# Loading the sixth wo column through 40 partitions in two groups of each layer

## The chip, the cores and the metric

The kernel runs on one core of a Trainium2 chip. The metric is the device time of one execution in microseconds (us); of several executions the median is taken. The profile is of one execution.

## What is computed

Two layers, with the same weights and caches in both. Each adds an attention over the last 4096 cached positions (one query, 32 heads of 192) and then a mixer and MLP to a vector of 640 numbers. The part that matters here is the attention and its output projection:

```python
W = min(4096, max(256, Sk // 4))                    # 4096
q = (x @ wq).reshape(B, Sq, Hq, Dh)                 # 1 x 640 @ 640 x 6144
scores = einsum("bhqd,bhkd->bhqk", q, k[-W:]) * Dh ** -0.5
o = einsum("bhqk,bhkd->bhqd", softmax(scores), v[-W:])
return o.reshape(B, Sq, Hq * Dh) @ wo               # 1 x 6144 @ 6144 x 640

x = x + attention(layernorm(x)); x = x + mixer(layernorm(x))   # layer 0
x = x + attention(layernorm(x)); x = x + mixer(layernorm(x))   # layer 1
```

## The kernel before

All data is bf16. The heads are worked off in eight groups of four (layer 0 from the last group to the first, layer 1 from the first to the last). Each head has a K and a V of 1.5 MB, each loaded by one transfer of 128 rows of 12,288 bytes (`load_k`, `load_v`). A group's part of wo is 768 rows of 640 numbers, 960 KB: partition p gets six consecutive rows of wo, 7,680 bytes, and so holds six columns of 640 numbers beside each other (`load_wo`, L161 to L169). All these land in eleven cells of SBUF. In layer 0 seven cells are gradually kept for the transposed K of heads 0 to 6, which layer 1 uses again.

Every load is issued by SP, in one order that is written out beforehand (`layer_stream`, L205 to L244): the K of the next group and the V of this one in turn, after them the group's wo, at the end of a layer w3 and w4 of the mixer. A load waits for its cell to be free and for one of eight DMA semaphores, so that at most eight transfers are in flight.

For a head, VectorE transposes K in quarters (L377), TensorE forms the scores (L453); after a group's four heads comes a softmax over all four (`softmax_steps`, L473 to L540), then TensorE multiplies with V (`pv`, L569), VectorE turns the result (L576), and `o_fold` (L578 to L589) leaves the group's outputs in `oT`, 128 partitions by six columns, which fit the six columns of wo.

The output projection of a group is done one group later, in the middle of the next softmax. In five groups of layer 0 and four of layer 1 it is done by `out_row` (L608 to L627): for each of the six columns two matmuls with one column of oT as weights and half a wo row as moving data, into rows 0 and 32 of a PSUM tile; `add` then adds these to a running sum `acc` in SBUF (L623, L625), and once per layer `turn_row` (L629 to L639) turns that row into a column. The other groups go through `out_proj` (L591).

The steps around it are in this order (`attention`, L766 to L801): T of the next head, `part_max`, T, S, `turn_max`, `full_max`, S, `spread_max`, the query projection of the group after next, `out_row`, `turn_p`, T, the rest of that projection, `add`, `swap` (the transposed probabilities PT, L523). The engines TensorE, VectorE, ScalarE and SP run in exactly this program order. Small PSUM tiles come from a pool of two buffers (`psm`), so a tile waits for the last reader of the tile but one before it.

Ahead of all that, 66 small matmuls (`WARM`, L77 and L310) run on TensorE, and constants are built: `ident`, `ones` (128 x 128, L264), `Lq` and others. The input x is loaded by one transfer of five partitions of 256 bytes (L127).

Of the kernel before, what the change touches and what calls it, by code (L numbers as in the profile page):

```python
# [8 lines left out]
BF16 = mybir.dt.bfloat16  # L9
F32 = mybir.dt.float32  # L10
# [7 lines left out]
P = 128  # L18
# [17 lines left out]
def kernel(  # L36
# [14 lines left out]
    nc = tc.nc  # L51
    _, _, D = A_x.shape
    _, H, Sk, Dh = A_k_cache.shape
# [20 lines left out]
    NA = Dh // 32  # L74
    NKX = 6
    NKEEP, NCELL = 7, 11
    WARM = 66  # L77

# [6 lines left out]
    assert W4C % 2 == 1 and W4C < NF  # L85
    GROUPS = [[list(range(h, h + QH)) for h in range(0, H, QH)] for _ in range(2)]
    GROUPS[0].reverse()

    head = ctx.enter_context(tc.tile_pool(name="head", bufs=1))
    fixed = ctx.enter_context(tc.tile_pool(name="fixed", bufs=1))  # L90
# [66 lines left out]
    def load_wq(layer, kc):  # L157
        nc.sync.dma_start(wq_sb[:, kc, :], A_wq[kc * P:(kc + 1) * P, :])
        return wq_sb

    def load_wo(layer, c):  # L161
        t = take(("wo", layer, c))
        src = A_wo[c * QC:(c + 1) * QC, :].rearrange("(p c) n -> p (c n)", c=NA)
        parts = {NG - 2: (3, 3), NG - 1: (3, 2, 1)}.get(c, (NA,)) if layer == 1 else (NA,)
        i = 0
        for n in parts:
            nc.sync.dma_start(t[:, i * D:(i + n) * D], src[:, i * D:(i + n) * D])
            i += n
        return t  # L169
# [91 lines left out]
        out=ident[:], in_=ident[:], compare_op=ALU.not_equal, fill=1.0,  # L261
        base=0, pattern=[[-1, P]], channel_multiplier=1,
    )
    ones = const.tile([P, P], F32, name="ones")  # L264
    nc.vector.memset(ones[:], 1.0)
    Lf = wx_sb[:, 0:2 * P].bitcast(F32).rearrange("p (j i) -> p j i", j=4)
    nc.gpsimd.memset(Lf, 0.0)
    for base in (0, -1, -64, -65):
# [22 lines left out]

    Lq = const.tile([P, 32], F32, name="Lq")
    nc.vector.reduce_sum(Lq[:], ident[:].rearrange("p (j a) -> p a j", j=4), axis=AX.X)
    eps1 = head.tile([P, 1], F32, name="eps1")
    nc.vector.memset(eps1[:], eps)

# [25 lines left out]
    def ln_center(x, rowsum):  # L322

        mean_ps = psm.tile([P, 1], F32, tag="psm")
        nc.tensor.matmul(mean_ps[:], lhsT=ones[:], rhs=rowsum[:, 0:1], start=True, stop=True)
        xc = big.tile([P, ND], BF16, name="xc")
        nc.vector.scalar_tensor_tensor(out=xc[:], in0=mean_ps[:, 0:1].broadcast_to([P, ND]), scalar=-1.0 / D,
                                       in1=x[:], op0=ALU.mult, op1=ALU.add)
        xcf = big.tile([P, ND], F32, name="xcf")
        nc.vector.scalar_tensor_tensor(out=xcf[:], in0=mean_ps[:, 0:1].broadcast_to([P, ND]), scalar=-1.0 / D,  # L330
                                       in1=x[:], op0=ALU.mult, op1=ALU.add)
        junk = sm.tile([P, ND], F32, tag="ln_junk")
        ssq = sm.tile([P, 1], F32, tag="ln_ssq")
        nc.scalar.activation(junk[:], xcf[:], ACTF.Square, accum_out=ssq[:, 0:1])

        def total():
            var_ps = psm.tile([P, 1], F32, tag="psm")
            nc.tensor.matmul(var_ps[:], lhsT=ones[:], rhs=ssq[:, 0:1], start=True, stop=True)
            return var_ps

        return xc, xcf, total
# [10 lines left out]
    def row_space(layer):  # L352

        t, i = ((wx_sb, 8 * P), (kx, 0))[layer]
        return t[0:33, i:i + D].bitcast(F32), t[0:33, i + D:i + D + QC // 2]

    kept = {}
    area = [None, 0]
# [114 lines left out]
    def softmax_steps(n, ST_ps, sc):  # L473
# [25 lines left out]
        def spread_max():  # L499
            nb_ps = psm.tile([P, 1], F32, tag="psm")  # L500
            nc.tensor.matmul(nb_ps[:], lhsT=held["w"],  # L501
                             rhs=ones[0:1, 0:1], start=True, stop=True)
            nb_sb = big.tile([P, 1], F32, name="nb_sb")
            nc.scalar.copy(nb_sb[:], nb_ps[:])  # L504
            Pr = o_bytes[:, 0:SW]
            lpart = big.tile([P, 1], F32, name="lpart")
            nc.scalar.activation(out=Pr, in_=ST_ps, func=ACTF.Exp,  # L507
                                 bias=nb_sb[:, 0:1], scale=sc[:, 0:1], accum_out=lpart[:, 0:1])
            held["Pr"], held["l"] = Pr, lpart
# [7 lines left out]
        def swap():  # L517
            ng = NGK // NT
            PT_ps = psm.tile([P, n, NJ4, NGK], F32, tag="psm")
            src = held["PrT"].rearrange("p (g j i) -> p i j g", g=ng, j=NJ4)  # L520
            for m in range(NM):
                for q in range(NT):
                    nc.tensor.matmul(PT_ps[32 * m:32 * (m + 1), :, :, ng * q:ng * (q + 1)], lhsT=Eq[:, q, :],  # L523
                                     rhs=src[:, m:QW:NM], start=True, stop=True)
            PT = big.tile([P, n, NJ4 * NGK], BF16, name="PT")
            nc.scalar.copy(PT[:].rearrange("p h c -> p (h c)"), PT_ps[:].rearrange("p h j g -> p (h j g)"))  # L526
            l_ps = psm.tile([P, QH], F32, tag="psm")
            nc.tensor.matmul(l_ps[:], lhsT=ones[:], rhs=held["lh"][:], start=True, stop=True)  # L528
            held["lps"] = l_ps
            return PT  # L530

# [73 lines left out]
                give(("wo", layer, c))  # L605
        return y_ps

    def out_row(layer, c, oT, acc, first):  # L608

        wo_t = need("wo", layer, c)  # L610
        N = D // 2
        yr_ps = psm.tile([33, N], F32, tag="psm")
        for k in range(NA):
            for i in range(2):
                nc.tensor.matmul(yr_ps[32 * i:32 * i + 1, :], lhsT=oT[:, k:k + 1],  # L615
                                 rhs=wo_t[:, k * D + i * N:k * D + (i + 1) * N], start=(k == 0), stop=(k == NA - 1))
        give(("wo", layer, c))

        def add():
            for i in range(2):  # L620
                r = slice(32 * i, 32 * i + 1)
                if first:
                    nc.vector.tensor_copy(acc[r, :], yr_ps[r, :])  # L623
                else:
                    nc.vector.tensor_add(acc[r, :], acc[r, :], yr_ps[r, :])  # L625

        return add  # L627

    def turn_row(acc):  # L629
        y_ps = psm.tile([P, ND], F32, tag="psm")  # L630
        N = D // 2
        for n in range(ND):
            a, b = n * P, (n + 1) * P
            for i in range(2):
                lo_, hi = max(a, i * N), min(b, (i + 1) * N)
                if lo_ < hi:
                    nc.tensor.matmul(y_ps[lo_ - a:hi - a, n:n + 1], lhsT=acc[:, lo_ - i * N:hi - i * N],  # L637
                                     rhs=ident[0:33, 32 * i:32 * i + 1], start=True, stop=True)
        return y_ps  # L639

    def attention(layer, x_cur, rs_cur, x_new, z_new, rs_new, ss_new):
# [29 lines left out]
        def add_y(y_ps, n):  # L671
            y_new = x_new if n == 0 else sm.tile([P, ND], F32, name="y_acc")
            if n == 1:

                rs = big.tile([P, 1], F32, name="rs_y")
                nc.vector.scalar_tensor_tensor(out=y_new[:], in0=y_ps[:], scalar=1.0, in1=y[0][:],
                                               op0=ALU.mult, op1=ALU.add, accum_out=rs[:, 0:1])

                def center():
                    nm_ps = psm.tile([P, 1], F32, tag="psm")  # L680
                    nc.tensor.matmul(nm_ps[:], lhsT=ones[:], rhs=rs[:, 0:1], start=True, stop=True)
# [12 lines left out]
            y[0] = y_new  # L694
# [39 lines left out]
        for gi, cur in enumerate(groups):  # L734
            nxt = list(enumerate(groups[gi + 1])) if gi + 1 < len(groups) else []
            ST_n = None
            if nxt:
# [24 lines left out]
                else:  # L762
# [5 lines left out]
                    part_max()  # L768
                    T(h0, 1)
                    S(h0, 0, ST_n, 0)  # L770
                    turn_max()
                    full_max()
                    S(h0, 1, ST_n, 0)
# [6 lines left out]
                        q[0]()  # L780
                    in_row = gi - 1 in rows
                    if pending is not None:
                        y_ps = out_row(layer, *pending, acc, gi - 1 == rows[0]) if in_row else out_proj(layer, pending)
                    turn_p()
                    T(h1, 0)
                    if q:
# [73 lines left out]
    def mixer(layer, x_cur, z, rs_cur, ss_cur, x_new, rs_new):  # L860
# [2 lines left out]


        s1_ps = psm.tile([P, 1], F32, tag="psm")
        nc.tensor.matmul(s1_ps[:], lhsT=ones[:], rhs=rs_cur[:, 0:1], start=True, stop=True)
        s2_ps = psm.tile([P, 1], F32, tag="psm")
        nc.tensor.matmul(s2_ps[:], lhsT=ones[:], rhs=ss_cur[:, 0:1], start=True, stop=True)
# [119 lines left out]
```

## Time and profile before

| | |
|---|---|
| median of three runs | 520.45 us (519.64 to 520.55) |
| the profiled execution | 519.84 us, its span 518.0 us |
| DMA read from memory | 216.47 MB, 418 GB/s over the span |
| TensorE matmuls, busy | 324.8 us (63%), granted clock 0.70 |
| VectorE, busy | 295.2 us (57%) |
| ScalarE, busy | 49.5 us (10%) |
| wo loads of 960 KB | 13, median 26.5 us from issue to landing |
| wo matmuls in out_row (L615) | 108, in 9 groups of 12 |

The span runs from the first to the last recorded instruction. In the profile PE is TensorE's matmuls, PEld its weight loads, DVE VectorE, ACT ScalarE, POOL GpSimd, SPq the queue of SP, which issues the loads. A line of the chain of waits has start, length and what the time went to; a line of the timeline has start, length, engine, line of the program, operation, what it writes and reads, its shape, how many, and in brackets how long the engine stood idle before it and for whom. A line of the list of waits says who waited for whom: us in total, times, longest. Section 3 of the page lists the DMA queues: q1 carries the data, q8 and q14 instructions.

### The profile page before, as it was taken

How to read it: one execution, taken by the hardware profiler on the slowest of the kernel's cores; microseconds unless marked ns; L12 is line 12 of the kernel's file. 1: busy time of each engine (PE TensorE's matmuls, PEld its weight loads, DVE VectorE, ACT ScalarE, POOL GpSimd, SP SyncE). 2: the span in 40 equal slices, each digit the busy share in tenths (PEclk: the TensorE clock that was granted, in tenths of full speed). 3: DMA queues.
4: the chain of work that ended last, by engine and by line, in shares of the span. 5: the costliest groups of instructions: out<-in, count | busy, mean ns of one | idle time of the engine just before them, and what ended most of it. 6: DMA issues, size and time to landing. Idle time of an engine off the chain costs nothing.

```text
span 518.0 us, 9589 instructions
## 1 busy us (share of the span) xinstructions
PE 324.8 (63%) x4146; PEld 192.6 (37%) x4146; DVE 295.2 (57%) x589; ACT 49.5 (10%) x175; POOL 4.0 (1%) x16
## 2 busy tenths in 40 slices
PE   2057656666664566767755866777566856648665
PEld 2024334333332334434333634434333433425334
DVE  2067667575584655656624356567675765664722
ACT  1000101010010100001011111001010101001011
POOL 2000000000000000000000000000000000000000
PEclk9999878565586755677665778557785676776855
DMA  8999999999999999999999999999999999999995
GB/s 347 433 425 426 433 426 427 432 428 425 433 426 427 431 426 429 428 426 431 424 425 396 385 426 429 428 428 428 429 426 427 432 428 426 426 434 426 427 416 235
DMA packets 23949, 217.08 MB, mean 419 GB/s; under 512 B 2532, under 2 KB 3044, under 8 KB 8420
## 3 DMA queue, kind: packets, MB, share of 16 engines
q1 hardware_dynamic: 23908, 216.48, 99.0%
q8 instruction: 32, 0.52, 0.4%
q14 instruction: 9, 0.07, 0.0%
HBM read 216.47 MB, written 0.00 MB: 418 GB/s over the span
## 4 chain that ended last, share of the span: by engine, by line
DMA 50%; PE 23%; DVE 22%; issue 2%; ACT 1%; SPq 1%; DVEq 0%; ACTq 0%
DMA cell<-in_A_k_cache_dram 39%; DVE cell L377 16%; DMA cell<-in_A_v_cache_dram 9%; PE ST_ps L453 9%; PE O_ps L569 7%; DVE o_sb L576 2%; DMA cell<-in_B_w_dram 2%; DVE pm L478 1%; PE nb_ps L501 1%; DVE o_sb L512 1%; ACT o_sb L507 1%; PE y_ps L637 1%; PE l_ps L528 1%; PE PT_ps L523 1%; PE qT_ps L407 1%
## 5 line engine op out<-in xcount | busy, mean ns | idle before, releaser
L453 PE MATMUL ST_ps<-cell,Qblk 128*16 128x256 bf16 x1536 | 163.7, 380 | 106.9 <-DVE cell L377 69.4
L377 DVE STREAM_TRANSPOSE cell<-cell 128x768 uint32<-128x768 uint32 x228 | 204.1, 945 | 15.2 <-DMA cell<-in_A_k_cache_dram 14.9
L453 PEld LDWEIGHTS <-Qblk 128*16 128x16 bf16 x1536 | 86.1, 111 | 176.5 <-issue 150.3
L569 PE MATMUL O_ps<-cell,PT 128*2 128x384 bf16 x1018 | 99.9, 461 | 8.2 <-DMA cell<-in_A_v_cache_dram 7.4
L576 DVE STREAM_TRANSPOSE o_sb<-O_ps 128x384 f32<-128x384 f32 x64 | 37.2, 581 | 111.8 <-PE O_ps L569 111.6
L569 PEld LDWEIGHTS <-PT 128*2 128x2 bf16 x1024 | 46.0, 100 | 22.1 <-issue 10.1
L512 DVE STREAM_TRANSPOSE o_sb<-o_sb 128x256 bf16<-128x256 bf16 x16 | 7.1, 446 | 33.2 <-ACT o_sb L507 24.2
L584 ACT ACTIVATE oT<-oT_ps,rl 32x6 bf16<-32x6 f32 x40 | 10.3, 258 | 164.0 <-PE oT_ps L583 157.8
L583 PEld LDWEIGHTS oT_ps<-o_sb,Lq 128*32 128x32 f32 x160 | 13.3, 145 | 19.3 <-issue 15.8
L583 PE MATMUL oT_ps<-o_sb,Lq 128*32 128x6 f32 x160 | 13.9, 195 | 10.4 <-DVE o_sb L576 9.9
L589 ACT ACTIVATE oT<-oT_ps,rl 32x6 bf16<-32x6 f32 x24 | 6.2, 258 | 107.6 <-PE ST_ps L453 87.1
L407 PE MATMUL qT_ps<-xc,wq_sb 128*128 128x1 bf16 x210 | 7.1, 165 | 12.8 <-DMA wq_sb<-in_A_wq_dram 12.0
L523 PE MATMUL PT_ps<-o_sb,Eq 128*32 128x32 bf16 x256 | 7.3, 237 | 9.3 <-DVE o_sb L512 4.1
L523 PEld LDWEIGHTS <-Eq 128*32 128x32 bf16 x256 | 5.4, 108 | 19.8 <-issue 19.7
L421 DVE TENSOR_TENSOR Xq<-qT_ps,maskq 128x24 bf16<-128x24 f32 (+1 forms) x18 | 2.8, 158 | 17.1 <-PE qT_ps L407 17.1
L396 PE MATMUL qr_ps<-wq_sb,xc 128*1 128x384 bf16 x90 | 12.1, 415 | 0.0
L407 PEld LDWEIGHTS <-wq_sb 128*128 128x128 bf16 x210 | 6.7, 102 | 14.0 <-DMA wq_sb<-in_A_wq_dram 13.0
L504 ACT COPY nb_sb<-nb_ps 128x1 f32<-128x1 f32 x16 | 2.5, 159 | 94.6 <-PE nb_ps L501 94.6
L615 PE MATMUL yr_ps<-cell,oT 128*1 128x320 bf16 x108 | 11.2, 355 | 0.0
L528 PE MATMUL l_ps<-lh,ones 128*128 128x4 f32 x32 | 7.7, 310 | 4.9 <-ACT PT L526 4.9
L428 PE MATMUL Qrep_ps<-Xq,Lb 128*128 128x24 bf16 (+1 forms) x18 | 3.2, 178 | 11.1 <-DVE Xq L421 10.8
L588 PE MATMUL oT_ps<-o,Lq 128*32 128x6 f32 x48 | 6.1, 199 | 6.5 <-DVE o L587 6.5
(143 smaller groups left out, 200.9 us busy)
## 6 DMA issues: line engine op xcount, KB each, us to landing
cell<-in_A_k_cache_dram SPq DMA_DIRECT2D x57, 1536.0 KB, 26.3
cell<-in_A_v_cache_dram SPq DMA_DIRECT2D x57, 1536.0 KB, 25.8
cell<-in_A_wo_dram SPq DMA_DIRECT2D x13, 960.0 KB, 26.5
wq_sb<-in_A_wq_dram SPq DMA_DIRECT2D x5, 1536.0 KB, 12.2
cell<-in_A_v_cache_dram SPq DMA_DIRECT2D x4, 768.0 KB, 23.8
cell<-in_A_v_cache_dram SPq DMA_DIRECT2D x2, 1248.0 KB, 11.5
cell<-in_B_w_dram SPq DMA_DIRECT2D x1, 1536.0 KB, 11.9
cell<-in_B_w_dram SPq DMA_DIRECT2D x2, 768.0 KB, 10.3
```

What stands on the lines that cost most here:

```text
L377: nc.vector.transpose(Tu, Ku[:, :, q * NY:(q + 1) * NY])
L396: nc.tensor.matmul(qr_ps[32 * i:32 * i + 1, :], lhsT=xc[:, kc:kc + 1], rhs=wq_sb[:, kc, t0 * P + i * N:t0 * P + (i + 1) * N], start=(kc == ...
L407: nc.tensor.matmul(qT_ps[:, tl:tl + 1], lhsT=wq_sb[:, kc, t * P:(t + 1) * P], rhs=xc[:, kc:kc + 1], start=(kc == 0), stop=(kc == ND - 1))
L453: nc.tensor.matmul(ST_ps[r:r + QW, :].rearrange("p (g i) -> p g i", g=ng), lhsT=Q[:, n, :], rhs=T4[:, :, f, :, t], start=(hq == 0 and n == ...
L512: nc.vector.transpose(held["PrT"], held["Pr"])
L523: nc.tensor.matmul(PT_ps[32 * m:32 * (m + 1), :, :, ng * q:ng * (q + 1)], lhsT=Eq[:, q, :], rhs=src[:, m:QW:NM], start=True, stop=True)
L528: nc.tensor.matmul(l_ps[:], lhsT=ones[:], rhs=held["lh"][:], start=True, stop=True)
L569: nc.tensor.matmul(O_ps[r:r + 2, :], lhsT=PT[:, hq, 2 * i:2 * i + 2], rhs=v_pair(V, h, 2 * i * Dh, 2 * Dh), start=(i < 4), stop=(i >= NB - 4))
L576: nc.vector.transpose(o_sb[:], O_ps.rearrange("p (e a c) -> p e c a", e=2, c=NA))
L583: nc.tensor.matmul(oT_ps[r, :], lhsT=Lq[:], rhs=o_sb[:, e, :, e], start=(e == 0), stop=(e == 1))
L584: nc.scalar.activation(oT[r, :], oT_ps[r, :], ACTF.Copy, scale=rl[r, 0:1])
L615: nc.tensor.matmul(yr_ps[32 * i:32 * i + 1, :], lhsT=oT[:, k:k + 1], rhs=wo_t[:, k * D + i * N:k * D + (i + 1) * N], start=(k == 0), stop= ...
```

## The change

Two groups of each layer (the third and fourth in order) get a wo whose sixth column is stored in another way. The first five columns go to all 128 partitions in one transfer as before, now with rows of 6,400 bytes. The sixth column, 128 pieces of 1,280 bytes, goes by two small transfers: 96 pieces to partitions 0 to 23, four beside each other, and 32 pieces to partitions 32 to 47, two beside each other. The sources of these are written with an outer dimension of 6 and of 4.

So that the outputs fit, `spread_low` takes the sixth column of oT through four selection matmuls into a tile of 48 partitions by four columns, and `out_row` then runs five column steps as before, four steps over partitions 0 to 23 and two over 32 to 47, the latter into PSUM rows 64 and 96. `add` has four rows to add, `acc` 97 partitions, and `turn_row` sums the two pairs of rows through `E2`. `ones` becomes one column that is read as a broadcast, and WARM goes from 66 to 14.

```diff
-    WARM = 66
+    WARM = 14
...
+    SPLIT = [{GROUPS[layer][g][0] // QH for g in gs} for layer, gs in enumerate(((2, 3), (2, 3)))]
+    NU = NA - 1
+    LOW = (0, 0, 6, 4), (3 * P // 4, 32, 4, 2)
...
+    def load_wo_split(t, src):
+        nc.sync.dma_start(t[:, 0:NU * D], src[:, 0:NU * D])
+        for row, at, ne, cols in LOW:
+            nc.sync.dma_start(t[at:at + 4 * ne, NU * D:(NU + cols) * D],
+                              src[row:row + 4 * ne * cols, NU * D:].rearrange("(j a) n -> a j n", a=ne))
...
+        if c in SPLIT[layer]:
+            load_wo_split(t, src)
+            return t
...
-    ones = const.tile([P, P], F32, name="ones")
-    nc.vector.memset(ones[:], 1.0)
+    one = const.tile([P, 1], F32, name="one")
+    nc.vector.memset(one[:], 1.0)
+    ones = one[:, 0:1].broadcast_to([P, P])
...
+    Sel = const.tile([P, 4, 48], BF16, name="Sel")
+    nc.gpsimd.memset(Sel[:], 0.0)
+    for row, at, ne, cols in LOW:
+        n = 4 * ne
+        nc.vector.tensor_copy(Sel[:, 0:cols, at:at + n].rearrange("p c (a b) -> p c a b", a=ne),
+                              ident[:, row:row + n * cols].rearrange("p (b c a) -> p c a b", b=4, c=cols))
+    E2 = const.tile([P, 2], F32, name="E2")
+    e4 = ident[:].rearrange("p (s i r) -> p s i r", s=2, i=2)
+    nc.vector.tensor_add(E2[:], e4[:, 0, :, 0], e4[:, 1, :, 0])
...
-        return t[0:33, i:i + D].bitcast(F32), t[0:33, i + D:i + D + QC // 2]
+        return t[0:97, i:i + D].bitcast(F32), t[0:33, i + D:i + D + QC // 2]
...
+    def spread_low(oT):
+        oX_ps = psm.tile([48, 4], F32, tag="psm")
+        for j in range(4):
+            nc.tensor.matmul(oX_ps[:, j:j + 1], lhsT=Sel[:, j], rhs=oT[:, NU:NA], start=True, stop=True)
+        oX = big.tile([48, 4], BF16, name="oX")
+        nc.scalar.copy(oX[:], oX_ps[:])
+        return oX
...
-        yr_ps = psm.tile([33, N], F32, tag="psm")
-        for k in range(NA):
+        yr_ps = psm.tile([33 if oX is None else 97, N], F32, tag="psm")
+        steps = [(0, oT[:, k:k + 1], wo_t[:, k * D:(k + 1) * D]) for k in range(NA if oX is None else NU)]
+        if oX is not None:
+            for _, at, ne, cols in LOW:
+                r = slice(at, at + 4 * ne)
+                steps += [(2 * at, oX[r, j:j + 1], wo_t[r, (NU + j) * D:(NU + j + 1) * D]) for j in range(cols)]
+        at = [r for r, _, _ in steps]
+        for k, (r, o, w) in enumerate(steps):
             for i in range(2):
-                nc.tensor.matmul(yr_ps[32 * i:32 * i + 1, :], lhsT=oT[:, k:k + 1],
-                                 rhs=wo_t[:, k * D + i * N:k * D + (i + 1) * N], start=(k == 0), stop=(k == NA - 1))
+                nc.tensor.matmul(yr_ps[r + 32 * i:r + 32 * i + 1, :], lhsT=o, rhs=w[:, i * N:(i + 1) * N],
+                                 start=r not in at[:k], stop=r not in at[k + 1:])
...
-            for i in range(2):
+            for i in range(2 if oX is None else 4):
...
-                                     rhs=ident[0:33, 32 * i:32 * i + 1], start=True, stop=True)
+                                     rhs=E2[0:97, i:i + 1], start=True, stop=True)
...
                     S(h0, 0, ST_n, 0)
+                    oX = None
+                    if pending is not None and pending[0] in SPLIT[layer]:
+                        oX = spread_low(pending[1])
                     turn_max()
```

More of the change, by code (lines that the diff above doesn't have):

```diff
@@ L324, in ln_center @@
         mean_ps = psm.tile([P, 1], F32, tag="psm")
-        nc.tensor.matmul(mean_ps[:], lhsT=ones[:], rhs=rowsum[:, 0:1], start=True, stop=True)
+        nc.tensor.matmul(mean_ps[:], lhsT=ones, rhs=rowsum[:, 0:1], start=True, stop=True)
         xc = big.tile([P, ND], BF16, name="xc")
@@ L337, in total @@
             var_ps = psm.tile([P, 1], F32, tag="psm")
-            nc.tensor.matmul(var_ps[:], lhsT=ones[:], rhs=ssq[:, 0:1], start=True, stop=True)
+            nc.tensor.matmul(var_ps[:], lhsT=ones, rhs=ssq[:, 0:1], start=True, stop=True)
             return var_ps
@@ L501, in spread_max @@
             nc.tensor.matmul(nb_ps[:], lhsT=held["w"],
-                             rhs=ones[0:1, 0:1], start=True, stop=True)
+                             rhs=one[0:1, 0:1], start=True, stop=True)
             nb_sb = big.tile([P, 1], F32, name="nb_sb")
@@ L527, in swap @@
             l_ps = psm.tile([P, QH], F32, tag="psm")
-            nc.tensor.matmul(l_ps[:], lhsT=ones[:], rhs=held["lh"][:], start=True, stop=True)
+            nc.tensor.matmul(l_ps[:], lhsT=ones, rhs=held["lh"][:], start=True, stop=True)
             held["lps"] = l_ps
@@ L606, in out_proj, with out_row @@
         return y_ps
-    def out_row(layer, c, oT, acc, first):
+    def spread_low(oT):
[5 more added lines that the diff above has]
+        return oX
+    def out_row(layer, c, oT, acc, first, oX=None):
         wo_t = need("wo", layer, c)
         N = D // 2
-        yr_ps = psm.tile([33, N], F32, tag="psm")
-        for k in range(NA):
+        yr_ps = psm.tile([33 if oX is None else 97, N], F32, tag="psm")
[6 more added lines that the diff above has]
+        for k, (r, o, w) in enumerate(steps):
             for i in range(2):
-                nc.tensor.matmul(yr_ps[32 * i:32 * i + 1, :], lhsT=oT[:, k:k + 1],
-                                 rhs=wo_t[:, k * D + i * N:k * D + (i + 1) * N], start=(k == 0), stop=(k == NA - 1))
+                nc.tensor.matmul(yr_ps[r + 32 * i:r + 32 * i + 1, :], lhsT=o, rhs=w[:, i * N:(i + 1) * N],
+                                 start=r not in at[:k], stop=r not in at[k + 1:])
         give(("wo", layer, c))
         def add():
-            for i in range(2):
+            for i in range(2 if oX is None else 4):
                 r = slice(32 * i, 32 * i + 1)
-                if first:
+                if first and i < 2:
                     nc.vector.tensor_copy(acc[r, :], yr_ps[r, :])
@@ L680, in center @@
                     nm_ps = psm.tile([P, 1], F32, tag="psm")
-                    nc.tensor.matmul(nm_ps[:], lhsT=ones[:], rhs=rs[:, 0:1], start=True, stop=True)
+                    nc.tensor.matmul(nm_ps[:], lhsT=ones, rhs=rs[:, 0:1], start=True, stop=True)
                     ym = big.tile([P, ND], F32, name="y_m")
@@ L782, in attention @@
                     if pending is not None:
-                        y_ps = out_row(layer, *pending, acc, gi - 1 == rows[0]) if in_row else out_proj(layer, pending)
+                        y_ps = out_row(layer, *pending, acc, gi - 1 == rows[0], oX) if in_row else out_proj(layer, pending)
                     turn_p()
@@ L865, in mixer @@
         s1_ps = psm.tile([P, 1], F32, tag="psm")
-        nc.tensor.matmul(s1_ps[:], lhsT=ones[:], rhs=rs_cur[:, 0:1], start=True, stop=True)
+        nc.tensor.matmul(s1_ps[:], lhsT=ones, rhs=rs_cur[:, 0:1], start=True, stop=True)
         s2_ps = psm.tile([P, 1], F32, tag="psm")
-        nc.tensor.matmul(s2_ps[:], lhsT=ones[:], rhs=ss_cur[:, 0:1], start=True, stop=True)
+        nc.tensor.matmul(s2_ps[:], lhsT=ones, rhs=ss_cur[:, 0:1], start=True, stop=True)
         def centred(dt, name):
```

## The prediction

> **What bounds the kernel now.** I read the page first, its DMA rows before its engines.
>
> ```profile
> span 518.0 us, 9589 instructions
> ...
> DMA  8999999999999999999999999999999999999995
> ...
> q1 hardware_dynamic: 23908, 216.48, 99.0%
> q8 instruction: 32, 0.52, 0.4%
> q14 instruction: 9, 0.07, 0.0%
> ```
>
> The sixteen DMA engines are busy in every slice but the first and last. No transfer of data goes away, so what can change is how the bytes lie on the engines. Beside the data queue, q8 and q14 fetch instructions, 0.59 MB in all.
>
> Second, the chain of waits, where it crosses from layer 0 to layer 1 and at the end, and SP's issues between.
>
> ```profile
> 265.46 11.56 DMA cell<-in_A_v_cache_dram
> 277.02 0.04 issue
> 277.06 0.81 PE O_ps L569 x8
> ```
> ```profile
> 283.69 3.39 SPq L145 DMA_DIRECT2D cell<-in_A_v_cache_dram  x2
> 291.01 2.94 SPq L132 DMA_DIRECT2D cell<-in_A_k_cache_dram  x2
> ```
> ```profile
> 500.70 10.35 DMA cell<-in_B_w_dram
> 511.05 0.05 issue
> 511.10 0.50 PE V_ps L901 x12
> ```
>
> Layer 0's last V lands at 277.02, and PE, idle before it, carries the chain on through out_proj, the mixer and layer 1's first scores. The k load at 291.01 waits for those scores to free a cell; by then most DMA engines have run dry. So layer 1's stream starts a fixed time after 277.02. At the end w3 lands at 511.05 and w4 at 514.68, and the rest hangs on them. A transfer lands when the slowest of its engines is done. **The kernel's time is therefore set by the slowest DMA engine twice: at 277.02 and at the end.**
>
> Third, the trace's DMA records. They don't name the engine, but each engine's share of a transfer ends in a 4-byte packet, 0.34 us before the landing, and from one to the next on the same engine it is 3.658 us for rows of 12,288 bytes, 2.302 for 7,680 and 0.420 for 1,280, to 1 or 2 ns. So each engine can be followed through a layer. Steps stand out: eight engines in fixed rotation fall back 1.417 us each time q8 fetches 16 KB, one engine 0.835 us at three of q14's 8 KB fetches in layer 0 (packets at 50.6, about 145 and 254.5), two others 0.55 to 0.59 us once. I call the one with three E7; the times of its fetches fit VectorE's instruction count (589), about 95 us apart. Where they stand, worked out from the records:
>
> ```
>                           end of layer 0's last V   end of last w4
> seven of the eight (q8)   276.10 to 276.68          513.10 to 514.36
> the eighth                275.18                    512.35
> E7 (q14, VectorE's)       276.00                    512.09
> other seven               273.37 to 273.94          510.61 to 512.17
> ```
>
> At the layer boundary the engines come nearly level again, so the second column is built up after 293 us.
>
> Which engines will carry the small transfers? The x load (5 partitions) puts its 256-byte packets on five engines: **E7, the two with a single q14 step and two with none; no q8 engine.** A transfer dealt in 6 or 4 parts (the outer dimension of the new sources) I take to run on sets nested with these five. Their order within the five the records don't give.
>
> The Trainium skill, "DMA: Bandwidth & Descriptors", section "Why a DMA increments its semaphore by 16 and not by 1", says that a HWDGE transfer uses the largest number of engines, up to 16, that divides both slowest dimensions, and the lowest-numbered ones; that would be engines 0 to 5 and 0 to 3, and the x load agrees as far as it goes.
>
> **The change, part by part.**
>
> *Main load.* Rows shrink from 7,680 to 6,400 bytes. Between the two lengths above a byte costs (3,658 - 2,302)/(8 x 4,608) = 0.0368 ns, so 8 x 1,280 x 0.0368 = 0.377 us less on every engine.
>
> *Small loads.* 96 + 32 packets of 1,280 bytes. The 160 KB loads of this trace have such packets: (420 - 9)/8 = 51.4 ns each. On six engines 16 each, on four of them 8 more. Four engines: 24 x 51.4 + 2 x 9 - 377 = +0.87 us per wo; two engines: +0.46; ten engines: -0.38. The packets cannot be cheaper than their bytes, 47 ns; as dear as 2,560-byte ones (102 ns in the trace) they would add 1.2 us more per wo.
>
> *Per layer, two such wo:* +1.75, +0.91 and -0.75 us.
>
> *Layer 0.* The q8 engines come to 276.68 - 0.75 = 275.93. If E7 is among the four, it comes to 276.00 + 1.75 = 277.75, **1.07 us after the old slowest**; as one of the two, 276.91 (+0.23); in neither, the gain is 0.75.
>
> *Layer 1.* The latest q8 engine comes to 513.61. E7 starts its two V at the boundary at 285.53 + 1.75 and is done at 294.60; the restart, 293.38 now by the first k load, moves with the chain to 294.45, so E7 starts 0.15 late and ends at 512.09 + 1.75 + 0.15 = 513.99: 0.37 us before the old 514.36.
>
> Of E7's three possible places I take the four engines: with nested sets they are four of the five x engines. Sum: +1.07 - 0.37 = **+0.7 us**. The ends are -0.75 - 0.75 = -1.5 (E7 in neither set) and, by the 102 ns packets, 0.7 + 4.8 = +5.5.
>
> *Instruction count.* WARM goes from 66 to 14: 52 matmuls out. Per split wo 4 selection matmuls and 22 instead of 12 in out_row: 56 in. PE's fetches on q8 stay as many, a few us later in layer 0. VectorE gets 3 instructions more in the head and 2 per split wo, about 11 of 589: E7's third fetch comes some 5 us earlier, still before 277. The warm matmuls lie before the first wq landing, which everything waits for.
>
> The Trainium skill, "Runtime: NRT & Kernel Launch", section "Instruction fetch mechanics", speaks against the whole idea: crossing a 16 KiB block of instructions costs one tail bump, mostly hidden. The 1.417 us steps say otherwise for a DMA-bound kernel; by the rule the engines would be level and the change would cost 2 x 1.75 = 3.5 us.
>
> *Compute.* The group with the first split wo in layer 0:
>
> ```profile
> 142.78 0.98 PE L615 MATMUL yr_ps<-cell,oT 128*1 128x320 bf16 x12
> ...
> 145.16 0.95 DVE L625 TENSOR_TENSOR wx_sb<-wx_sb,yr_ps 1x320 f32<-1x320 f32 x2
> ...
> 146.16 0.45 PE L523 MATMUL PT_ps<-o_sb,Eq 128*32 128x32 bf16 x16 [0.70 <-DVE wx_sb L625]
> ```
>
> Twelve matmuls in pairs take 0.98 us, a pair 0.135 (0.267 where the clock is halved, as at 407.75). Five pairs more: 0.67 or 1.33 us. Four narrow matmuls and the ACT copy ahead of turn_max: some 0.4 us by the 0.30 of L417's six. Two adds more: 0.95. VectorE's adds already hold back PT, so the group runs 1.35 us later at full clock, up to 2.8 at half: queued behind them are swap, PV and the V cells that SP waits for. What hides it is VectorE's waiting for K:
>
> ```profile
> DVE cell L377 <- DMA cell<-in_A_k_cache_dram: 5.4, 3, 2.4
> ```
> ```profile
> DVE cell L377 <- DMA cell<-in_A_k_cache_dram: 3.0, 2, 1.9
> ```
>
> The first is 165 to 205 us, the second 420 to 470: against 2.7 to 5.6 us in layer 0 (where PE then waits another 3.6 at 277) and 1.35 + 2.8 in layer 1 (with 2.2 us of waits for w3 behind). DMA has 16 to 29 us of issued work there and does not run dry. Cost taken: nothing; without the cover, 1 to 2.5 us.
>
> *The rest.* Sel and E2 in the head lie under the first 20 us of loads. `ones` as a broadcast column: same instructions, same count. wo is loaded at 132 and 164 and first used at 143 and 174, so a later part has 10 us. SP issues two DMAs more per split wo, 0.33 us each in a queue that mostly waits; they take 2 of the 8 in flight, 6 x 3.66 us remain. turn_row's 97 rows instead of 33: bounded by a 33x128 f32 weight load of 0.32 and a 128x128 one of 0.31, so nothing.
>
> **Against the median.** The profiled execution took 519.84 (518.0 span and 1.8 around it); the median of three is 520.45. I add +0.7 to the median: **521.2 us**.
>
> **Rivals.**
> - *Relief.* The small transfers miss E7, or give it the 16 packets. For it: ten of sixteen engines are relieved, all eight q8 engines among them. Against it: E7 is one of the five of the x load. Time 520.45 - 1.5 = 519.0, or with 16 packets +0.23 - 0.75 = 519.9.
> - *Later at another place (slower).* The softmax step of the four split groups: VectorE's adds ahead of PT. It decides where the clock is halved in both groups of layer 1, since 5.6 us then exceed the 3.0 of K waits and the 2.2 at w3; price 1 to 2.5 us on top, 522 to 523.6. Dearer packets end there too.
> - *The change does not steer.* The small transfers are dealt to all sixteen engines: 128/16 = 8 packets, 0.43 against 0.38 us, 4 x 0.05 = +0.2, 520.65.
>
> **How the numbers follow.** About 0.2%, 1.04 us, is what a measurement of this kernel can tell from no change. Forecast, chance 0.55: 521.2, own range 520.2 to 522.2 (restart order and clock move it by several tenths): faster 0.03, same 0.30, slower 0.22. Relief 0.22: faster 0.17, same 0.05. Late compute or dear packets 0.18: slower. No steering 0.05: same. Together faster 0.20, same 0.40, slower 0.40. The range runs from full relief, 519.0, to 522.9 inside the late case; the rest above it is left out.
>
> **What would show it.** Layer 0's last V landing: later than 277.02 by about 1 us if right, near 276.3 if relief. From there to the first k issue of layer 1 it should stay 14.0 us. E7's 4-byte packets should be the last of the sixteen at that V, q8's engines 1.8 us before. From that issue to w4's last landing it is 223.7 us now and should be some 0.4 less. PT's wait for L625 grows by about 1 us in four groups, K waits after 165 and 420 shrink. It is wrong if E7 is not last, if 1,280-byte packets take other than 51 to 55 ns, or if DMA slices fall below 9 between 300 and 490 us.

## The result and the profile after

The changed kernel takes 521.01 us (median of 22 runs, 520.63 to 523.53), the kernel before, run beside it, 520.02 us (22 runs). The ratio is 1.0020, 95% interval 1.0012 to 1.0027: **about 1.0 us slower**. The forecast was +0.7 us. The profiled execution took 521.19 us, 1.35 us more than that of before.

The page of the changed kernel shows more DMA packets; the bytes and the fetches of instructions are the same.

```profile
span 519.3 us, 9620 instructions
...
DMA packets 24501, 217.08 MB, mean 418 GB/s; under 512 B 2572, under 2 KB 3596, under 8 KB 8972
...
q1 hardware_dynamic: 24460, 216.48, 99.0%
q8 instruction: 32, 0.52, 0.4%
q14 instruction: 9, 0.07, 0.0%
```

q1 has 23,908 packets before and 24,460 now: 552 more. 512 of them are the small pieces (4 x 128), the other 40 are 4 bytes long: 4 x (6 + 4), one for each engine that a small transfer uses. So the transfers run on six and on four engines, as the prediction took them to. That is also what the rule on the number of engines in the Trainium skill, "DMA: Bandwidth & Descriptors", section "Why a DMA increments its semaphore by 16 and not by 1", gives, which the prediction named.

Now the three places that the prediction pointed at: the chain of waits at layer 0's last V, SP's issues behind it (start, length, line, operation), and the chain at the end.

```profile
266.27 11.72 DMA cell<-in_A_v_cache_dram
278.00 0.04 issue
278.04 0.81 PE O_ps L592 x6
```
```profile
284.67 3.38 SPq L148 DMA_DIRECT2D cell<-in_A_v_cache_dram  x2
291.97 3.75 SPq L135 DMA_DIRECT2D cell<-in_A_k_cache_dram  x2
```
```profile
501.97 10.34 DMA cell<-in_B_w_dram
512.31 0.05 issue
512.35 0.49 PE V_ps L942 x12
```

The last V lands at 278.00 where it was 277.02: **0.98 us later**. From there to layer 1's first k issue it is 13.97 us (13.99 before), so the delay is handed on whole. w3 lands at 512.31 where it was 511.05: 1.26 us later. What layer 0 lost was not won back in layer 1.

Followed from transfer to transfer as in the prediction (worked out from the trace's DMA records), the sixteen engines end layer 0's last V like this; the column of before is the prediction's, with the fifth engine of q8's rotation set apart:

```
                                     before             after
E7 (VectorE's instructions)          276.00             277.66
fifth in q8's rotation               276.14             277.20
the other seven of q8                275.18 to 276.68   up to 276.27
the engines with no fetch on q8      273.37 to 273.94   from 274.36
```

E7 is last and sets the landing (0.34 us after its 4-byte packet). It moved by 1.66 us; the prediction had 1.75. The seven of q8 are 1.4 us and more ahead of it. One engine of q8, the fifth in its rotation, is not relieved but loaded: it moved by 1.06 us and is second. The two don't come to the first split wo as they did before: followed back from these packets, E7 ends the load ahead of it 0.10 us earlier (128.65 against 128.76) and the fifth 0.14 later (129.29 against 129.15). From there on they lost 1.76 and 0.92 us, where 24 and 16 packets per wo were to cost 1.75 and 0.91.

The softmax step of a split group got longer just as far as its rows said. Rows of the groups between 168 and 182 us of the changed kernel (count, then busy us and mean ns, then idle time before and its cause):

```profile
L663 DVE TENSOR_TENSOR wx_sb<-wx_sb,yr_ps 1x320 f32<-1x320 f32 x4 | 1.9, 481 | 0.0
...
L653 PE MATMUL yr_ps<-cell,oT 128*1 128x320 bf16 x10 | 0.9, 303 | 0.0
L653 PE MATMUL yr_ps<-cell,oX 24*1 24x320 bf16 (+1 forms) x12 | 0.7, 293 | 0.0
...
L546 PE MATMUL PT_ps<-o_sb,Eq 128*32 128x32 bf16 x16 | 0.5, 240 | 1.7 <-DVE wx_sb L663 1.7
```

PT waits 1.7 us for the adds, 0.70 before. Where the time went can be read in the list of waits: of VectorE's three waits for K between 165 and 205 us, 5.4 us in all, one is left, and of the 3.0 us between 420 and 470 none.

```profile
DVE cell L400 <- DMA cell<-in_A_k_cache_dram: 1.5, 1, 1.5
```

So the added compute ate VectorE's idle time, and the cover is nearly used up.

### The profile page after: what moved, and what is told of

It is laid out like the page before. It is cut to its first block, busy times and chain, and to the rows that moved or that the text cites. A ratio compares the mean times of both kernels' runs of the same rounds, so it can differ in the third digit from the quotient of the medians.

```text
span 519.3 us, 9620 instructions
## 1 busy us (share of the span) xinstructions
PE 330.4 (64%) x4150; PEld 193.0 (37%) x4150; DVE 298.8 (58%) x600; ACT 50.0 (10%) x179; POOL 4.2 (1%) x17
## 3 DMA queue, kind: packets, MB, share of 16 engines
q1 hardware_dynamic: 24460, 216.48, 99.0%
## 4 chain that ended last, share of the span: by engine, by line
DMA 36%; PE 33%; DVE 25%; issue 4%; ACT 1%; SPq 1%; DVEq 0%; ACTq 0%
DVE cell L400 18%; DMA cell<-in_A_v_cache_dram 18%; DMA cell<-in_A_k_cache_dram 14%; PE ST_ps L476 12%; PE O_ps L592 10%; DVE o_sb L599 2%; DMA cell<-in_B_w_dram 2%; DMA kx<-in_A_v_cache_dram 2%; PE qr_ps L419 1%; PE nb_ps L524 1%; PE PT_ps L546 1%; PE l_ps L551 1%; PE yr_ps L653 1%; DVE kx L663 1%; PE y_ps L675 1%
## 5 line engine op out<-in xcount | busy, mean ns | idle before, releaser
L476 PEld LDWEIGHTS <-Qblk 128*16 128x16 bf16 x1536 | 84.3, 112 | 174.8 <-issue 147.4
L592 PE MATMUL O_ps<-cell,PT 128*2 128x384 bf16 x1018 | 101.0, 466 | 7.9 <-DMA cell<-in_A_v_cache_dram 7.0
L419 PE MATMUL qr_ps<-wq_sb,xc 128*1 128x384 bf16 x90 | 14.0, 468 | 0.0
L551 PE MATMUL l_ps<-lh,one 128*128 128x4 f32 x32 | 8.0, 321 | 4.9 <-ACT PT L549 4.9
L524 PEld LDWEIGHTS nb_ps<-one,o_sb 1*128 1x128 f32 x32 | 7.3, 281 | 7.4 <-issue 5.5
```

Source lines behind the costliest of these rows:

```text
L419: nc.tensor.matmul(qr_ps[32 * i:32 * i + 1, :], lhsT=xc[:, kc:kc + 1], rhs=wq_sb[:, kc, t0 * P + i * N:t0 * P + (i + 1) * N], start=(kc == ...
L476: nc.tensor.matmul(ST_ps[r:r + QW, :].rearrange("p (g i) -> p g i", g=ng), lhsT=Q[:, n, :], rhs=T4[:, :, f, :, t], start=(hq == 0 and n == ...
L524: nc.tensor.matmul(nb_ps[:], lhsT=held["w"], rhs=one[0:1, 0:1], start=True, stop=True)
L551: nc.tensor.matmul(l_ps[:], lhsT=ones, rhs=held["lh"][:], start=True, stop=True)
L592: nc.tensor.matmul(O_ps[r:r + 2, :], lhsT=PT[:, hq, 2 * i:2 * i + 2], rhs=v_pair(V, h, 2 * i * Dh, 2 * Dh), start=(i < 4), stop=(i >= NB - 4))
```

## The experiments

The theory is that the time is set by the slowest DMA engine, E7 in layer 0, because it gets small packets on top of VectorE's instruction fetches. The rival that ended on the slower side was compute: the longer softmax step in four groups.

### Compute alone, loads alone by layer

`compute_only` keeps the loads of before and all instructions of the change.

```diff
-        if c in SPLIT[layer]:
-            load_wo_split(t, src)
-            return t
...
-                steps += [(2 * at, oX[r, j:j + 1], wo_t[r, (NU + j) * D:(NU + j + 1) * D]) for j in range(cols)]
+                steps += [(2 * at, oX[r, j:j + 1], wo_t[r, j * D:(j + 1) * D]) for j in range(cols)]
```

> All wo are loaded as in the kernel before (six columns, 128 rows each, no small transfers), but the instructions of the change stay: the selection matmuls, the copy, ten matmuls more per split wo, four adds in place of two, WARM = 14. The part of oT that the selection reorders is multiplied with other columns of wo than it should be, so this part of the output projection is not the reference's. Theory (the slowest DMA engine sets the time, and where the bytes lie is what changed): within 0.2 us of the kernel before; layer 0's last V lands at 277.0 +- 0.2 after the span's start. Rival (the longer softmax step in the split groups costs the time): all of the +1.0 us stays. Between them: a part of it.

Measured: 520.55 against 520.41 us, ratio 1.0004 (0.9991 to 1.0016). The chain at layer 0's last V:

```profile
265.48 11.71 DMA cell<-in_A_v_cache_dram
277.19 0.04 issue
277.23 0.81 PE O_ps L589 x8
```

The V lands at 277.19, not at 278.00. The selection, the copy, ten matmuls and two adds more per group, and 52 warm matmuls less, move nothing that a median can tell; a cost of 1.0 us lies outside the interval. The compute rival falls.

`layer0_only` and `layer1_only` split in one layer.

```diff
-    ... enumerate(((2, 3), (2, 3)))]
+    ... enumerate(((2, 3), ()))]        # layer0_only
+    ... enumerate(((), (2, 3)))]        # layer1_only
```

> The split loads and their instructions in layer 0 alone. Theory: layer 0's term is the whole cost, because E7 is last at layer 0's last V: that V lands at 278.0 (+1.0), and the time is +0.9 to +1.1 us; layer 1 then loads as before and adds nothing but the order in which its engines restart. If layer 1's split is what costs (its engines come later at w4), this kernel is at 0 to +0.3 us. If compute costs in each group by itself: +0.5 us.

Measured: 521.31 against 520.41 us, ratio 1.0017 (1.0007 to 1.0027): +0.9 us, nearly all of the change. The last V lands at 278.14, with E7's packet at 277.77 and the fifth q8 engine's at 277.35. The landing moves as in the change.

> The split loads and their instructions in layer 1 alone. Theory: layer 0 is as before (last V at 277.0 +- 0.2), and in layer 1 the q8 engines are relieved by 0.75 us while E7 comes to 513.8 against 514.4 for the slowest: -0.4 us, and 0 if the order in which the engines restart after the boundary eats it. If layer 1's split costs: +0.3 us or more. If each split group costs compute: +0.5 us.

Measured: 521.27 against 520.55 us, ratio 1.0016 (1.0002 to 1.0029). The last V lands at 277.21, as it should. But the time is not 0.4 us less: the interval begins 0.1 us above the kernel before. Its profiled execution was its fastest (520.29 us), so the trace doesn't show what the others lost. The stretch from layer 1's first k issue to the last 4-byte packet of w4 doesn't help either. Where layer 1 loads as before it is 223.35 (before), 223.37 (`compute_only`) and 224.00 us (`layer0_only`), where it is split 223.64 (the change) and 223.12 (`layer1_only`). It differs by 0.9 us from trace to trace, more than the term in question. One cause is seen in the traces: at the boundary the engines stop, and the spread of their first k shares behind it is 1.9 us before (297.04 to 298.95) and 2.3 in the change (298.03 to 300.31), in another order each time. So layer 1's term is settled only this far: the gain of 0.37 us isn't there. By the medians alone the two layers can't be told apart, +0.9 and +0.7 us, together 0.6 more than the change; it is the landing of layer 0's last V that shows what layer 0 costs.

### One fetch more on E7, and one less

Both keep the change's loads and alter only how many instructions VectorE has had by a certain time.

```diff
+        for _ in range(more):                          # dve_more: 5 per head of layer 0
+            nc.vector.memset(pad[:], 0.0)
```

> The change with five one-column memsets more on VectorE per head of layer 0 (about 130 in all; each takes 0.06 us and lies in time in which VectorE waits). In the change the fetches on the queue q14 that slow E7 come when VectorE has issued 66, 191, 321, 447 and 575 instructions, that is one per 128, and the fourth comes at 337 us, in layer 1. With 130 more the fourth comes at about 250 us, before layer 0's last V. Theory (E7 is last there, and it is VectorE's instruction engine): E7 comes to 277.66 + 0.84 = 278.5, that V lands at 278.8, and the time is 0.8 us above the change, +1.6 to +2.0 us above the kernel before. If E7 isn't what the last V waits for, or these fetches aren't VectorE's: as the change, +1.0 us.

Measured: 522.57 against 520.47 us, ratio 1.0047 (1.0033 to 1.0061): +2.1 us, 1.1 more than the change. q14 has two fetches more in the whole kernel, and the last V lands at 278.76:

```profile
q14 instruction: 11, 0.09, 0.0%
```
```profile
267.54 11.22 DMA cell<-in_A_v_cache_dram
278.76 0.04 issue
278.80 0.81 PE O_ps L592 x8
```

E7's packet is at 278.36, the next engine's at 277.24. The memsets write four bytes per partition of a tile that nothing reads; they move no data by DMA. What they did is bring VectorE's fourth fetch from 337 to 255.0 us. The landing is 0.76 us later for one fetch of 0.835: **E7 is the engine that the last V waits for, and its fetches are VectorE's.** The timed loss is somewhat more than the landing (1.1 against 0.76 us), which the two intervals allow.

```diff
-            nc.vector.tensor_scalar(out=lh[:], ...         # dve_less, with eleven of the head alike
+            nc.gpsimd.tensor_scalar(out=lh[:], ...
-                o_fold(h, oT, rl, len(groups) - 4 > gi >= 2 * layer)
+                o_fold(h, oT, rl, layer == 1 and len(groups) - 4 > gi >= 2 * layer)
```

> The change with 34 instructions less on VectorE up to 250 us: eleven of the head and the seven small multiplications of the softmax step go to GpSimd, and in layer 0 the sixteen additions of o2 become a second matmul each. The fetch that comes when VectorE has issued 321 instructions then moves from 247.5 to about 280 us, behind layer 0's last V. Theory: E7 comes to 277.66 - 0.84 = 276.8, the last is then the engine that q8 uses fifth in its rotation and that has 16 packets per split wo, at 277.2; that V lands at 277.5 in place of 278.0, and the time is 0.2 to 0.5 us below the change, +0.5 to +0.8 us above the kernel before. If E7 isn't the last one there: 278.0 as in the change.

This one missed its aim. The fetch moved from 247.5 to 265.3 us only, not past the V, and so the V lands at 278.05, as in the change. In the three kernels the fetches come when VectorE has started 64 to 66, 190 to 193, 316 to 321 and 442 to 447 of the instructions that the trace records, however these lie in time; by 265 us only 25 of the 34 had been saved (318 started, 343 in the change). The timed runs (524.15 us, 523.26 to 526.01 but for the profiled one at 520.53) are 3.7 us above the kernel before; the profiled one doesn't show why, and this stays open. (The kernel also has one fetch more on q8, 33, and one on q14, 10.)

### The same packets, spread

Three kernels were to take the weight off E7 by dealing the same 128 packets to other engines.

```diff
-    LOW = (0, 0, 6, 4), (3 * P // 4, 32, 4, 2)      # row, partition, outer dimension, columns
+    # spread:    outer dimensions 24 and 16
+    # three:     outer dimensions 3 (8 partitions each) and 16
+    # no_steer:  one transfer, outer dimension 16 (2 partitions each), 4 columns
```

> The change with its instructions and its bytes unchanged; only the outer dimension of the two small sources is 24 and 16 in place of 6 and 4, so that the 128 packets lie on 12 and 16 engines. By 51.4 ns a packet: twelve engines get 8 + 2 packets per wo, 0.42 + 0.11 - 0.38 = +0.16 us, four get 0.11 - 0.38 = -0.27. Theory: in layer 0 the slowest engine of the instruction queue q8 is late by 2 x 0.16 = 0.3 us if it is one of the twelve, E7 comes to 276.3 and not to 277.7; total +0.1 to +0.4 us, and where the four relieved engines are the late ones of q8, 0 or below. Rival (instructions, waits of the longer group, two DMAs more in SP's queue): stays at +1.0 us or more.

> The first small source gets an outer dimension of 3 (24 partitions x 4 columns, 32 packets on each of three engines), the second one of 16 (2 packets on each of 16 engines). It shows which of the lowest engines E7 is. Three engines get 32 x 51.4 + 9 + 2 x 51.4 + 9 - 377 = +1.39 us per wo, thirteen 0.11 - 0.38 = -0.27 us. If E7 is one of the three: it comes to 276.0 + 2.8 = 278.8 at layer 0's last V, 2.1 us after the slowest of before; time +1.5 to +2.5 us. If it is not: the three come to at most 273.9 + 2.8 = 276.7, the q8 engines to 276.2, the last V lands 0 to 0.5 us earlier; in layer 1 the three come to 513.4 to 515.0 against 514.36 before; time -0.8 to +0.5 us. Rival (compute): +1.0 us in any case.

> One small transfer per split wo, of all 128 rows, with an outer dimension of 16: 32 partitions x 4 columns, 8 packets of 1,280 bytes on each of the sixteen engines; two adds per group as in the kernel before. Theory: 8 x 51.4 + 9 - 377 = +0.04 us per wo on every engine, +0.2 us for the four; no engine is favoured, so layer 0's last V lands at 277.0 to 277.2 and the time is 0 to +0.4 us. If what made the kernels 'spread' and 'three' slow (all packets of all engines took up to twice as long while the small transfers were under way) comes with any small transfer over sixteen engines, this one loses about 1 us per wo as well: +4 us. Then it says nothing about steering.

Measured: `spread` 1.0097 (1.0081 to 1.0113), `three` 1.0058 (1.0045 to 1.0072), `no_steer` 1.0124 (1.0108 to 1.0140), that is +5.2, +3.0 and +6.0 us. All three missed on the slow side, and not by their packets' number: while their small transfers are under way, every packet of every engine is slow. Two more kernels looked for the part that does it.

> The change with its first small transfer as it is (outer dimension 6) and only the second one dealt over sixteen engines, two packets each. One look, for the packets' durations. If the transfer over sixteen engines is what slowed all packets in 'spread' and 'three', the 12,288-byte packets behind it take up to 0.9 us in place of 0.46 here too, and the time is 2 to 4 us above the kernel before. If it was the first transfers of those kernels (12 engines, or 32 packets on three), this one runs at 0.46 us per packet, and the time is +0.2 to +0.6 us (E7 gets 16 + 2 packets or 2).

Measured: 521.44 us in its one execution, of which a small difference can't be read. Its 12,288-byte packets behind the first split wo take 0.46 us, a few up to 0.6 at the end. So the second transfer isn't what costs 1 us per wo.

> One wo per layer is split, not two; the first small source has an outer dimension of 3 (32 packets on each of three engines), the second one of 2 (16 packets on each of two). E7 got the small packets in the change, where 4 engines are used; followed through 'three' it seems not to be among the lowest three. Theory with E7 outside: thirteen engines get -0.38 us per layer; the three get 32 x 51.4 + 9 - 377 = +1.28, two of them +2.10, and come from 273.9 to at most 276.1 at layer 0's last V, behind the slowest q8 engine at 276.30: that V lands 0.3 to 0.4 us earlier (276.6 to 276.7), and the time is -0.2 to -0.75 us. If E7 is among the three or the two: it comes to 277.3 or 278.1, +0.6 to +1.4 us. Rival (compute, half the groups): +0.5 us.

Measured: 522.14 against 520.55 us, ratio 1.0037 (1.0023 to 1.0051). The packets are slow here too (12,288 bytes in up to 0.97 us), so this says nothing on E7's place; whether the weight could be kept off E7 wasn't settled.

Then the order of the source rows and the places in the tile were told apart.

```diff
-    ....rearrange("(j a) n -> a j n", a=ne)          # no_steer
+    ....rearrange("(a j) n -> a j n", a=ne)          # no_steer_order: eight adjacent rows per engine
```
```diff
+        if c in SPLIT[layer]:                        # plain_split: the kernel before, five columns and one
+            parts = NA - 1, 1
```

> The kernel 'no_steer' (128 packets of 1,280 bytes, 8 on each of sixteen engines, the same places in the tile) with one difference: each engine reads eight adjacent rows of wo, where it read every sixteenth. If the order of the source rows is what made all packets slow in 'no_steer', 'three', 'spread' and 'not_e7', packets take 0.055 and 0.46 us here, layer 0's last V lands at 277.0 to 277.3 and the time is 0 to +0.4 us: the even deal costs nothing and wins nothing. If the number of engines or the places in the tile do it, it stays at +6 us.

> The kernel before with one difference: the four wo that the change splits are loaded as five columns and one, both to all 128 partitions (no selection, no other matmuls). Each of sixteen engines gets 8 packets of 1,280 bytes, read in the same order as in 'no_steer_order', but written to 128 partitions x 1 column in place of 32 x 4. If the places in the tile are what made all packets slow there, packets take 0.055 and 0.46 us here, the last V of layer 0 lands at 277.0 to 277.3, and the time is 0 to +0.4 us (4 x 0.04 us of data, by the theory that the even deal wins and costs nothing). If a short transfer over sixteen engines is what makes them slow, it is 4 to 6 us above the kernel before.

Measured: `no_steer_order` 1.0099 (1.0086 to 1.0112), +5.1 us; `plain_split` 520.34 against 520.18 us, ratio 1.0003 (0.9993 to 1.0013). In both, sixteen engines read the same pieces of wo, eight each; one writes them to 32 partitions, the other to 128. Which rows each engine reads in `plain_split` the records don't show. The stretches around the first split wo (bounds, length, busy time and count of PE, PEld, DVE, ACT and POOL, then PE's clock, the DMA share and GB/s), of `no_steer_order`, of `plain_split` and of the change:

```profile
130.00:131.00 1.00, 0.72 (x8) 0.25 (x5) 0.68 (x2) 0.00 (x0) 0.00 (x0) 0.50 1.30 367
131.00:132.00 1.00, 1.00 (x21) 0.77 (x19) 0.00 (x0) 0.00 (x0) 0.00 (x0) 0.50 0.87 261
132.00:133.00 1.00, 1.00 (x15) 0.55 (x7) 0.00 (x0) 0.26 (x1) 0.00 (x0) 0.50 1.24 377
```
```profile
130.00:131.00 1.00, 0.43 (x8) 0.37 (x10) 1.00 (x2) 0.00 (x0) 0.00 (x0) 1.00 1.05 432
131.00:132.00 1.00, 0.81 (x8) 0.19 (x4) 1.00 (x2) 0.00 (x0) 0.00 (x0) 0.53 1.04 434
132.00:133.00 1.00, 0.71 (x10) 0.50 (x11) 0.29 (x2) 0.00 (x0) 0.00 (x0) 0.50 1.18 498
```
```profile
130.00:131.00 1.00, 1.00 (x12) 0.58 (x10) 1.00 (x2) 0.00 (x0) 0.00 (x0) 0.50 1.15 469
131.00:132.00 1.00, 0.72 (x8) 0.25 (x5) 0.62 (x2) 0.00 (x0) 0.00 (x0) 0.50 1.05 440
132.00:133.00 1.00, 1.00 (x20) 0.82 (x19) 0.00 (x0) 0.00 (x0) 0.00 (x0) 0.50 1.06 455
```

The reader is to see the last two columns together: the DMA engines are as busy in the first block as in the others, but move 261 to 377 GB/s in place of 432 to 498. Busy time with few bytes is how slow packets look. `plain_split` is also the even deal done cleanly: 8 packets on each engine win nothing and lose nothing. (Its last V lands at 277.79, later than expected, with packets at full speed. The engine that is last there is the seventh in q8's rotation. It ends the load ahead of the first split wo 0.68 us later than in the kernel before, 128.84 against 128.16, and the trace doesn't show why; from there on it lost 0.09 us, which is what two even deals at 0.04 were to cost.)

## Why the prediction was right, and where it was not

- **What bounds the kernel: right.** The last V's landing moved by 0.98 us, its distance to the first k issue stayed (13.97 us), and a kernel with the split in layer 0 alone has the same landing and nearly the whole loss.
- **E7 among the four engines: right.** E7 was put at 277.75 and stands at 277.66, last of sixteen, and its two split wo cost it 1.76 us against 1.75. Adding one fetch to it moved the landing again.
- **Packets and rows: right.** A share of six-engine transfers takes 0.834 us = 16 x 51.6 + 9 ns, one of four 0.420, and the 6,400-byte rows 1.926 us against 2.302: 0.376 less, 0.377 predicted.
- **All eight q8 engines relieved: wrong.** The five engines of the x load hold no q8 engine, that was right; but the sixth engine of the six-engine transfer is the fifth in q8's rotation. It got +0.46 us per wo, not -0.38, and came to 277.20, 0.46 us before E7, where the prediction let every engine of q8 end by 275.93, 1.8 us before it. In layer 0 it doesn't set the landing and costs nothing. At the end of layer 1 it is at 515.35 and E7 at 515.36; the last engine, at 515.61, is neither of them, but, followed the same way, the second in q8's rotation, which gets no small packets.
- **Layer 1, -0.37: the term that was mis-sized.** The stretch of layer 1 is 0.29 us longer in the profile, not 0.4 shorter, and `layer1_only` is 0.1 to 1.5 us above the kernel before. The relief itself was there. The second engine of q8's rotation is the last at w4 in both traces; from the end of its first k share behind the boundary to its last packet it took 216.06 us before (298.30 to 514.36) and 215.31 in the change (300.31 to 515.61), 0.75 less, as predicted. But it restarted 2.01 us later. Of this 0.98 is the later landing; the other 1.03 is the order in which the engines restart, and this the prediction took to stay nearly as it was. That holds for this pair of traces. In the trace of `layer1_only` the stretch is 0.23 us shorter than before, so the term changes with the restart, and what it is in the median the runs don't show.
- **The number: near, in part by luck.** The whole result, +1.0, is about layer 0's term alone, +0.98 where +1.07 was put; the sum of +0.7 is near because the term that failed is small. And 521.2 lies close to the 521.01 measured because it was added to a median of three, 520.45, while the kernel before took 520.02 beside the change.
- **Compute hidden: right, with little to spare.** PT's wait grew by 1.0 us as sized, K waits fell from 5.4 to 1.5 us and from 3.0 to nothing, and the compute by itself measures 1.0004 (0.9991 to 1.0016).
- **Instruction count: right.** q8 has 32 fetches as before; E7's third comes 7 us earlier (247.5 against 254.5; 5 were predicted) and before the V.
- **The rivals.** Relief fell because E7 gets 24 packets per wo and not none. No steering fell because six and four engines are used; `plain_split` shows what it would have given.

The page "Runtime: NRT & Kernel Launch" of the Trainium skill, section "Instruction fetch mechanics", named in the prediction, has the crossing of a block of instructions mostly hidden. `dve_more` is against it for this kernel: 0.76 us at the landing for one fetch.

## What to carry to other kernels

In a kernel whose DMA engines are all busy, a landing is the slowest engine's: before moving bytes between engines, find which engines also fetch instructions and which of them is last at each point where everything stops, since relief for ten engines is worth nothing if the eleventh was nearly as late. Follow single engines through the small packets that end their shares; the mean rate and the DMA rows of the page look the same in both kernels. When a small load is written to a part of the partitions only, look at its packets' durations too, for it may slow every other load.

## What the hardware showed that was not expected

**Small loads to few partitions slowed everything.** 12,288-byte packets take 0.46 us. In `no_steer_order` they took up to 1.0 us, 1,280-byte ones up to 0.13 instead of 0.055, on all engines, for about 3 us per split wo, and 4 wo cost 5.1 us. The number of engines and the size are those of `plain_split`, which has none of it; two orders of reading, that of `no_steer` and that of `no_steer_order`, are both slow; and the added instructions alone cost nothing (`compute_only`). That leaves the places written as the cause there. In `three` and `not_e7` the first transfer writes the same 24 partitions as the change, from three engines with eight partitions each, and it is slow; in the change each engine writes four neighbouring ones, and it is not. So it isn't the number of partitions alone, but which engine writes which.

The Trainium skill, "SBUF — State Buffer", section "Door 1: The DMA port swizzle", puts partitions in groups of four on sixteen ports, 32 partitions apart on the same one; and "DMA: Bandwidth & Descriptors", section "The descriptor swizzle", gives each engine of a 128-partition load one port of its own. If the shares of a small transfer lie on the engines in order, which no run shows, then in the change every small transfer writes four neighbouring partitions per engine, which by these pages are the engine's own port; in `spread`, `no_steer` and `no_steer_order` two engines meet on a port, in `three` and `not_e7` an engine goes over two ports, its neighbours' among them. "Back-pressure in remote DMA" on the latter page says that a full port holds up the engines behind it, of another kind of transfer. The second transfer of `six_sixteen` has four engines on a port, for two packets each, and its packets are slow only at the end and a little. This fits all eight layouts that ran, but it is argued and not shown; a run made to test it, such as three engines on their own four partitions, wasn't tried.

**Instruction fetches follow the instruction count.** VectorE's fetch on E7 comes about every 128 recorded instructions, at the same counts in three kernels with 669, 703 and 851 of them, and costs its engine some 0.84 us each time.
